# An attention and MLP block on one core: the residual of three output chunks added by accumulating transfers, VectorE's exponential groups allowed to begin during gelu, and a new list of their places

## The chip, the cores and the metric

The kernel runs on one core of a Trainium2 chip (trn2). The metric is device time in microseconds (us), the median of several runs. Before the change it is 464.41 us (9 runs, 464.27 to 464.72). A core has TensorE (PE, matmuls), VectorE (DVE), ScalarE (ACT), GpSimd (POOL) and SyncE (SP, which here only issues transfers). Each engine works through its own list of instructions in order and waits for the others by semaphores.

## The reference, cut to what matters

```
x: [1, 2048, 448]                 # S = 2048 rows, D = 448
xn = layernorm(x)
s  = MHA(xn): 16 heads of 28; p = softmax(q k^T * 28**-0.5); (p v) merged @ wo
g  = silu(gelu(xn @ w1 + b1) @ w2 + b2)        # hidden size 1792
out = x + s * g                                # bfloat16
```

## The kernel before, in words

The 2048 query rows are cut into C = 4 chunks of 512, the 16 heads into G = 4 groups of four. A block is one head group with one chunk; there are 16, and block b has group b // 4 and chunk b % 4. A block has 64 score tiles m of 128 keys by 512 queries, one for each head and each of 16 key tiles; a tile fills one PSUM bank. Block 15 is cut further into parts of 256, 128 and 128 queries.

**The exponential of the scores is the bulk of the work, and two engines share it.** ScalarE does most tiles: TensorE writes the scores of the next unit into a ring of six PSUM banks (`t_score`, the matmul is recorded at L1210), in units that alternate between three banks (from bank 0) and two (from bank 4), and ScalarE turns a unit into bfloat16 probabilities in one instruction of 1536 or 1024 columns (`p_exps`, L1266). So the scores of a unit can start when the exponential two units earlier has left the banks. The destination is `P`, or, when they are free, pieces of `h` and `xnT`; the profile names the groups by these.

VectorE does the tiles named in `QUADS`: 33 numbers q, each for the four tiles m = 4q to 4q + 3. Such a group takes its scores from whatever single bank is free (one of the pool: `misc`, `acc`, ring bank 3 or 2 at times); VectorE evicts each of the four (L1366), and then makes the exponential of the group out of integer and float16 operations on 2048 columns (`p_expq`, L1417 to L1424: three of about 0.69 us and two of about 1.22 us). A late score is either joined to a score burst that is due anyway (it then uses rows of the array that the burst leaves free) or issued by itself. The P·V matmuls (`pv_task`, L1478) accumulate in the bank `acc`, with VectorE's groups slipped in when they are ready.

**Beside this run** the projections of q, k and v for later groups (L734, L1021), the first MLP layer (L1062, L1079) and, from the middle on, gelu (`p_gelu`, L1117). In the gelu stretch ScalarE stops taking exponentials and alternates between pieces of `h` in SBUF and seven direct pieces of three PSUM banks each, which TensorE fills in the score ring (`p_direct`). Then follow the second layer (L1138, evicted with its bias by L1143), silu as a tanh (L1153) and a product (L1157), which leave `g` in `h`.

**When a block ends**, `p_epi` copies `acc` (L1536), sums with a matmul (L1543), takes the reciprocal (L1546, tile `rc`), splits it on POOL into a high and a low bfloat16 part (L1548 `rhi`, L1549 `rlo`), spreads it by a matmul (L1558) and multiplies (L1565). The last three parts of block 15 go through `p_epi4` and `p_norm4` instead: cast L1510, row sums by a matmul L1521, reciprocal L1524, product L1527.

**The output** of a chunk is made once its last block is normalised: `p_out` and `p_last` multiply with wo (`t_wo`, L1575, in parts of head groups), and `t_oev` finishes each 128-row tile on VectorE: times `g` (L1584), plus x (L1586), into `osb`, a part of `h`. The x for this comes from `x2`, another part of `h`, which SP loads again after silu of the chunk (L1162), because the first copy of x has been given to VectorE's groups as room. Chunks 0 to 2 leave by two transfers of two tiles each (L1592), chunk 3 by one for each tile (L1590), all issued on SP. For the last tile of chunk 3 silu is finished late: tanh on ScalarE after the last exponential (L1167), then a multiply and an add on POOL (L1169, L1171).

**What sets the order.** All of this is written by a planner in the kernel's own source, at build time: each strand of work is a generator that yields tasks (engine, buffers read and written, an assumed duration, a priority), and `run` always puts down the task that could start first by these durations, the priority deciding between near ones. What comes out is a fixed order for each engine. `p_late` decides when VectorE's groups start: group q waits for

```
K.next_m >= m0 - LEAD and len(K.banks) > 0 and K.unit_of(b, 3) is not None
```

where `next_m` is the next tile of ScalarE's stream, m0 = 4q and LEAD = 0. During gelu `next_m` stands still. `p_busy` (L895) puts filler matmuls into `acc` where the planner finds TensorE idle for too long.

Of the kernel before, what the change touches and what calls it, by code (L numbers as in the profile page):

```python
# [19 lines left out]
C = 4  # L20
# [7 lines left out]
MTOT = NBLK * T * 4  # L28

GM = 64 * 9 + 6  # L30
QUADS = (17, 19, 21, 35, 37, 50, 55, 68, 75, 84, 90, 102, 107, 116, 121, 133, 136, 146, 147, 149, 151, 162, 165, 179, 186, 195, 201, 209, 214, 218, 229, 235, 244)
SM_SCALE = DH ** -0.5
LOG2E = 1.4426950408889634
EXP_A3, EXP_A2, EXP_LC = 0.16391228, 0.00783292, 1.1187538523466403
# [9 lines left out]
SEM, OWN = 0.07, 0.03  # L44
SWITCH = 0.1
JOINT = 0.05
LEAD, WAIT = 0, 3.0
EPS = 0.1


# [23 lines left out]
class _Kernel:  # L74
# [183 lines left out]
    def alloc(self):  # L258
# [100 lines left out]
        self.b_fsb, self.b_sig = [B(), B()], [B(), B()]  # L359
        self.b_hf = [[B() for _ in range(FT)] for _ in range(C)]  # L360
        self.b_dum = B()
        hx = lambda c, f0, n: self.h[:, c, 512 * f0:512 * (f0 + n)].rearrange("p (k n) -> p k n", n=512)
        self.pslots = [(self.P[:, i0:i0 + n, :], k) for i0, n in ((0, NP),) for k in range(n)]
        self.pslots += [(hx(2, 5, 9), k) for k in range(9)] + [(hx(3, 0, 12), k) for k in range(12)]
# [218 lines left out]
    def loads(self):  # L583
        K = self

        def ld(dst, src, sem, w, land):
            return K.dma(SP, lambda eng: eng.dma_start(dst, src), sem, writes=w, land=land)
        xr = K.A_x[0].rearrange("(c p t) d -> c p t d", p=128, t=4)
        wq = K.A_wqkv
        ld(K.x_sb[:, 0, 0:2, :], xr[0][:, 0:2, :], K.s_x[0], [K.b_x0[0]], 3.2)  # L590
        K.dma(ACT, lambda eng: eng.dma_start(K.x_sb[:, 0, 2:4, :], xr[0][:, 2:4, :]), K.s_x0b, writes=[K.b_x0[1]], land=3.9)
        K.dma(ACT, lambda eng: eng.dma_start(K.x_sb[:, 1, :, :], xr[1]), K.s_x[1], writes=[K.b_x[1]], land=6.5)
        sv = K.stg.rearrange("p k w h d -> p k w (h d)")
        wqk = wq[:, 0:2 * D].rearrange("r (w n) -> r w n", w=2)

        def lw(n0, n1, sem, tok, land):
            for k in range(KT):
                rows = slice(128 * k, min(128 * k + 128, D))
                ld(sv[0:rows.stop - rows.start, k, :, n0:n1], wqk[rows, :, n0:n1], sem, [tok] if k == KT - 1 else [], land)
        lw(0, 4 * DH, K.s_w["wqk"], K.b_stg, 6.1)  # L600
        ld(K.wv[:, 0:3, 0:D], wq[0:384, 2 * D:3 * D].rearrange("(kt p) n -> p kt n", p=128), K.s_w["wv"], [], 0)
        ld(K.wv[0:64, 3, 0:D], wq[384:448, 2 * D:3 * D], K.s_w["wv"], [K.b_wv], 10.3)
        for c in (2, 3):
            ld(K.x_sb[:, c, :, :], xr[c], K.s_x[c], [K.b_x[c]], 8.0 + 1.8 * c)
        lw(4 * DH, D, K.s_wqk1, K.b_stg1, 16.5)

        ld(K.b2b[:, :], K.B_b2.partition_broadcast(128), K.s_w["b"], [K.b_b2], 20)
        ld(K.w1[:, 0:3, :], K.B_w1[0:384, :].rearrange("(kt p) f -> p kt f", p=128), K.s_w["w1"], [], 0)
        ld(K.w1[0:64, 3, :], K.B_w1[384:448, :], K.s_w["w1"], [K.b_w1], 30)

        def late_w2():
            yield ("until", lambda: K.next_m >= 64 * 2 * C and all(u in K.free_u for u in (4, 5, 6)))
            K.free_u = [u for u in K.free_u if u not in (4, 5, 6)]
            for u in (4, 5, 6):
                for b in K.b_U[u]:
                    K.b_w2.r += b.r + [b.w]
            ld(K.w2[:, :, :], K.B_w2.rearrange("(ft p) d -> p ft d", p=128), K.s_w["w2"], [K.b_w2], K.now + 14)
        K.spawn(late_w2(), 50)

        def pool_pads():  # L620
            yield ("until", lambda: K.stg_done == 2)
            yield _Task(POOL, lambda eng: eng.memset(K.wo[:, :, :], 0.0), [], [K.b_wo], 1.6)
            K.wait(SP, K.b_wo.w)
            K.b_wo.w = None
            for hh in range(H):
                g, j = hh // 4, hh % 4
                ld(K.wo[32 * j:32 * j + DH, g, :], K.A_wo[hh * DH:(hh + 1) * DH, :], K.s_w["wo"],
                   [K.b_wo] if hh == H - 1 else [], 45)
        K.spawn(pool_pads(), 50)
# [518 lines left out]
    def p_silu(self, c):  # L1148
        K = self
        yield ("until", lambda: K.f2n[c] == 4 and K.ready([K.b_fsb[c % 2]], 0.3) and (c < 2 or K.g_done[c - 2]))  # L1150
        fb, sg = K.fsb[:, c % 2, :, :], K.sig[:, c % 2, :, :]
        nt = 4 if c < C - 1 else 3
        yield _Task(ACT, lambda eng: eng.activation(sg[:, 0:nt, :], fb[:, 0:nt, :], ACTF.Tanh, scale=0.5),  # L1153
                    [K.b_fsb[c % 2]], [K.b_sig[c % 2]], 0.1 + 0.375 * nt, 0.0, 0)
        for t0 in range(0, nt, 2):
            t1 = min(t0 + 2, nt)
            yield _Task(DVE, lambda eng, t0=t0, t1=t1: eng.scalar_tensor_tensor(  # L1157
                K.g_sb[:, c, t0:t1, :], sg[:, t0:t1, :], 1.0, fb[:, t0:t1, :], op0=ALU.add, op1=ALU.mult),
                        [K.b_sig[c % 2], K.b_fsb[c % 2]], [K.b_h[c], K.b_g[c]], 0.15 + 0.467 * (t1 - t0), 0.0, 3)
        K.g_done[c] = True  # L1160
        K.b_x2[c].r = list(K.b_h[c].r) + [K.b_h[c].w]
        K.dma(SP, lambda eng: eng.dma_start(K.x2[:, c, :, :], K.A_x[0].rearrange("(c p t) d -> c p t d", p=128, t=4)[c]),  # L1162
              K.s_x2[c], writes=[K.b_x2[c]])
        if nt < 4:
            yield ("until", lambda: K.exp_m == MTOT - 1)
            o = K.g_sb[:, c, 3, :]
            yield _Task(ACT, lambda eng: eng.activation(sg[:, 3, :], fb[:, 3, :], ACTF.Tanh, scale=0.5),  # L1167
                        [K.b_fsb[c % 2]], [K.b_sig3], 0.47, 0.0, 0)
            yield _Task(POOL, lambda eng: eng.tensor_tensor(o, sg[:, 3, :], fb[:, 3, :], ALU.mult),  # L1169
                        [K.b_sig3, K.b_fsb[c % 2]], [K.b_h[c], K.b_g3], 0.85, 0.05, 0)  # L1170
            yield _Task(POOL, lambda eng: eng.tensor_tensor(o, o, fb[:, 3, :], ALU.add),  # L1171
                        [K.b_fsb[c % 2]], [K.b_h[c], K.b_g3], 0.85, 0.05, 0)
# [151 lines left out]
    def join(self, r):  # L1324
# [8 lines left out]
        p["task"].fn, p["task"].reads, p["task"].writes = t.fn, t.reads, t.writes  # L1333
        p["task"].dur, p["task"].rows = t.dur, t.rows

    def p_late(self):
        K = self
        yield ("until", lambda: K.late_on)
        K.spawn(K.p_room(), 0)
        for q in QUADS:  # L1340
            m0 = 4 * q
            b = K.sub_of(m0)
            yield ("until", lambda: K.next_m >= m0 - LEAD and len(K.banks) > 0 and K.unit_of(b, 3) is not None)
            u = K.unit_of(b)
            K.free_u.remove(u)
            ms = list(range(m0, m0 + 4))
            left = list(ms)
            for k in range(4):
                bank, tok = yield ("bank",)
                r = {"bank": bank, "tok": tok, "left": left, "m": None, "done": False}  # L1350
                still = lambda: (K.gu is not None and K.exp_u >= K.gu - 1 and K.dir_read < len(DIRECT)) or K.next_m >= MTOT or K.now > t0 + WAIT
                t0 = max(K.now, tok.tr, tok.tw or 0.0)
                yield ("until", lambda: K.may_join(r) or still())
                if K.may_join(r):
                    K.join(r)
                    yield ("until", lambda: r["done"])
                else:
                    r["m"] = left.pop(0)
                    yield K.t_score([r["m"]], {r["m"]: bank}, [tok], 0.9)
                K.spawn(K.p_apass(u, m0, r["m"] - m0, bank, tok), m0)  # L1360
            K.spawn(K.p_expq(m0, u), m0)
# [218 lines left out]
    def t_oev(self, ps, tok, c, t):  # L1580
        K = self
        o = K.osb[:, c, t, :]
        wr = K.b_osb[c][t // 2] if c < C - 1 else K.b_o4[t]
        yield _Task(DVE, lambda eng: eng.tensor_tensor(o, ps, K.g_sb[:, c, t, :], ALU.mult),  # L1584
                    [tok, K.b_g3 if (c, t) == (C - 1, 3) else K.b_g[c]], [wr], 0.63, 0.0, 3)
        yield _Task(DVE, lambda eng: eng.tensor_tensor(o, o, K.x2[:, c, t, :], ALU.add),  # L1586
                    [K.b_x2[c], wr], [wr], 0.4, 0.0, 3)
        ov = K.out[0].rearrange("(c p t) d -> c p t d", p=128, t=4)[c]
        if c == C - 1:
            K.outs.append(K.dma(SP, lambda eng: eng.dma_start(ov[:, t, :], o), K.s_out[6 + t], reads=[wr]))  # L1590
        elif t % 2:
            K.outs.append(K.dma(SP, lambda eng: eng.dma_start(ov[:, t - 1:t + 1, :], K.osb[:, c, t - 1:t + 1, :]),  # L1592
                                K.s_out[2 * c + t // 2], reads=[wr]))

    def p_out(self, c, t):
        K = self
        bank, tok = yield ("bank", lambda: K.on_done[(G - 1) * C + c] and K.g_done[c])
# [68 lines left out]
```

## Time and profile before

| | |
|---|---|
| median of 9 runs | 464.41 us |
| the profiled execution, its own time | 464.32 us |
| its span in the profile | 462.5 us |
| granted TensorE clock, mean | 0.998 |
| exponentials of 1536 columns on ScalarE (L1266) | 166, about 1.5 us each in the profile |
| exponentials of 1024 columns on ScalarE (L1266) | 197, about 1.07 us each |
| gelu stretch on ScalarE | 250.3 to 277.3 us |
| evictions of VectorE's groups (L1366) | 0.69 us each |
| residual adds on VectorE (L1586) | 16, 0.39 us in the median |
| output products on VectorE (L1584) | 16, 0.62 us |

A duration in the profile runs from the start of an instruction to its end, and the next one on the engine can start before that end; so the distance of two starts is the better price of an exponential. Idle time before an instruction is shown in square brackets with what ended it. "<-" separates what is written from what is read. POOL's and the transfers' queues have their own rows (SPq, ACTq). In the list of groups, three numbers in a row stand for the shortest, the median and the longest of them, in ns.

### The profile page before, as it was taken

To read this page: it belongs to the slowest core of one execution; us is meant where nothing else is said; L and a number is where in the kernel's file an instruction comes from. 1 tells how busy PE (TensorE), PEld (TensorE's weight loads), DVE (VectorE), ACT (ScalarE), POOL (GpSimd) and SP (SyncE) were. 2 spreads that over 40 slices of the span, in tenths; PEclk is the share of its full clock that TensorE was granted. 3 is DMA by queue.
4 is the path that set the end of the run, shared out by engine and by line. 5 is a ranking of instruction groups with operands and counts; after the bars stand their busy time and mean duration, and the time that the engine had idled before them with its cause. 6 is when DMAs were issued, how large, how long until landed. Compare 5 with 4: busy or idle time off the path is not lost.

```text
span 462.5 us, 10781 instructions
## 1 busy us (share of the span) xinstructions
PE 435.2 (94%) x4524; PEld 169.6 (37%) x4555; DVE 372.4 (81%) x588; ACT 448.3 (97%) x407; POOL 37.8 (8%) x79
## 2 busy tenths in 40 slices
PE   5999999999999899999999999999999999999995
PEld 4533333333323232323233343333333344343562
DVE  8956898898879797988888844889469698888796
ACT  6999999999999999999999999999999999999994
POOL 7470000001000000100000010000000001000001
PEclk9999999999999999999999999999999999999999
DMA  8501000000000000000040000101000010100001
GB/s 266 148 2 37 2 1 0 3 1 3 2 1 1 0 3 1 2 1 2 1 140 1 1 1 0 42 2 41 0 10 32 1 41 4 40 1 21 23 23 61
DMA packets 8385, 11.17 MB, mean 24 GB/s; under 512 B 1697, under 2 KB 6993, under 8 KB 8338
## 3 DMA queue, kind: packets, MB, share of 16 engines
q1 hardware_dynamic: 8050, 9.80, 6.9%
q8 instruction: 36, 0.59, 0.5%
q10 hardware_dynamic: 288, 0.69, 0.4%
q14 instruction: 11, 0.09, 0.1%
HBM read 8.61 MB, written 1.84 MB: 23 GB/s over the span
## 4 chain that ended last, share of the span: by engine, by line
PE 51%; ACT 36%; issue 10%; DVE 3%; DMA 1%; POOL 0%; ACTq 0%; DVEq 0%; POOLq 0%
ACT P L1266 17%; PE ring L1210 14%; ACT h L1266 12%; PE acc L1478 10%; ACT xnT L1266 6%; PE ring L1079 6%; PE misc L1138 5%; PE ring L1138 4%; PE acc L895 3%; PE misc L1079 2%; PE ring L734 2%; PE misc L734 1%; PE misc L1210 1%; PE ring L1575 1%; DMA x_sb<-in_A_x_dram 1%
## 5 line engine op out<-in xcount | busy, mean ns | idle before, releaser
L1266 ACT ACTIVATE P<-ring 128x1024 bf16<-128x1024 f32 (+1 forms) x194 | 222.0, 1256 | 1.8 <-PE ring L1210 0.9
L1210 PE MATMUL ring<-qT,kT 32*128 32x512 bf16 (+2 forms) x1088 | 143.7, 358 | 12.9 <-ACT P L1266 5.5
L1266 ACT ACTIVATE h<-ring 128x1024 bf16<-128x1024 f32 (+1 forms) x97 | 114.3, 1290 | 0.2
L1210 PEld LDWEIGHTS ring<-qT,kT 32*128 32x128 bf16 x1088 | 37.1, 91 | 132.6 <-ACT P L1266 53.6
L1266 ACT ACTIVATE xnT<-ring 128x1536 bf16<-128x1536 f32 (+1 forms) x72 | 83.5, 1282 | 0.2 <-PE misc L1210 0.2
L1478 PE MATMUL acc<-P,vaug 128*32 128x512 bf16 (+2 forms) x535 | 47.5, 358 | 0.0
L895 PE MATMUL acc<-ident,zero 128*128 128x128 bf16 x525 | 41.5, 220 | 0.0
L1079 PE MATMUL ring<-xnT,w 128*128 128x512 bf16 x149 | 39.1, 381 | 1.4 <-issue 1.0
L1548 POOL CAST rhi<-rc 128x16 bf16<-128x16 f32 x15 | 6.6, 440 | 389.2 <-DVE rc L1546 344.3
L895 PEld LDWEIGHTS acc<-ident,zero 128*128 128x128 bf16 x525 | 29.7, 98 | 17.6 <-issue 16.8
L1138 PE MATMUL misc<-w,h 128*128 128x448 bf16 x126 | 30.1, 355 | 0.0
L1478 PE MATMUL acc<-h,vaug 128*32 128x512 bf16 x241 | 25.1, 384 | 0.0
L1210 PE MATMUL misc<-qT,kT 32*128 32x512 bf16 (+1 forms) x64 | 24.1, 379 | 0.0
L1138 PE MATMUL ring<-w,h 128*128 128x448 bf16 x98 | 22.3, 354 | 0.1
L1366 DVE TENSOR_SCALAR x_sb<-ring 128x512 uint16<-128x512 f32 x22 | 15.2, 689 | 7.6 <-PE ring L1210 7.2
L1536 DVE CAST E_sb<-acc 128x512 bf16<-128x512 f32 x15 | 10.4, 692 | 13.2 <-PE acc L1478 13.0
L1079 PEld LDWEIGHTS ring<-xnT,w 128*128 128x128 bf16 x160 | 12.8, 97 | 18.7 <-issue 5.2
L1478 PE MATMUL acc<-xnT,vaug 128*32 128x512 bf16 (+2 forms) x240 | 18.2, 330 | 0.0
L1079 PE MATMUL misc<-xnT,w 128*128 128x512 bf16 x57 | 16.9, 382 | 0.9 <-issue 0.8
L1366 DVE TENSOR_SCALAR w<-ring 128x512 uint16<-128x512 f32 x20 | 13.8, 688 | 4.0 <-PE ring L1210 4.0
L1478 PEld LDWEIGHTS acc<-P,vaug 128*32 128x32 bf16 x535 | 11.9, 95 | 13.8 <-issue 10.2
L1117 ACT ACTIVATE h<-h 128x2560 bf16<-128x2560 bf16 (+2 forms) x8 | 16.6, 2072 | 0.0
(278 smaller groups left out, 654.9 us busy)
## 6 DMA issues: line engine op xcount, KB each, us to landing
h<-in_A_x_dram SPq DMA_DIRECT2D x4, 448.0 KB, 3.3
w<-in_B_w_dram SPq DMA_DIRECT2D x1, 1568.0 KB, 7.2
w<-in_B_w_dram SPq DMA_DIRECT2D x1, 1344.0 KB, 9.2
out_dram<-h SPq DMA_DIRECT2D x6, 224.0 KB, 1.9
x_sb<-in_A_x_dram SPq DMA_DIRECT2D x2, 448.0 KB, 4.7
h<-in_A_wqkv_dram SPq DMA_DIRECT2D x3, 168.0 KB, 4.7
x_sb<-in_A_x_dram ACTq DMA_DIRECT2D x1, 448.0 KB, 4.2
out_dram<-h SPq DMA_DIRECT2D x4, 112.0 KB, 1.7
```

The costliest lines, as they stand in the source:

```text
L734: ins = eng.matmul(bank, w[:, kt, g * 128:(g + 1) * 128], K.xnT[:, kt, c * 512:(c + 1) * 512], start=(kt == 0), stop=(kt == KT - 1))
L895: ins = eng.matmul(K.acc[:, 0:128], K.zero[:, :], K.ident[:, :], start=False, stop=True, skip_group_check=True)
L1079: ins = eng.matmul(bank, K.w1[:, kt, ft * 128:(ft + 1) * 128], K.xnT[:, kt, c * 512:(c + 1) * 512], start=(kt == 0), stop=(kt == KT - 1))
L1117: yield _Task(ACT, lambda eng, dst=dst, src=src: eng.activation(dst, src, ACTF.Gelu_apprx_tanh), rd, K.b_hf[c][f0:f0 + n] + ([K.b_h[c]] if ...
L1138: ins = eng.matmul(ps, hv[:, ft, t * 128:(t + 1) * 128], K.w2[:, ft, :], start=(ft == 0), stop=(ft == FT - 1))
L1210: return eng.matmul(dst, K.kT[32 * j:32 * j + 32, g, t * 128:(t + 1) * 128], K.qT[32 * j:32 * j + 32, g, c * 512 + q0:c * 512 + q0 + nq], ...
L1266: return eng.activation(reg[:, i0:i0 + n, :], K.ring[:, b0:b0 + n, :], ACTF.Exp, scale=SM_SCALE)
L1366: yield _Task(DVE, lambda eng: eng.tensor_scalar(K.unit[u][:, 512 * k:512 * k + 512].bitcast(dt.uint16), bank, SM_SCALE * LOG2E * 128.0, ( ...
L1478: return eng.matmul(K.acc[32 * j:32 * j + 32, q0:q0 + nq], K.vaug[:, t, 4 * g + j, :], ap[:, col:col + nq], tile_position=(0, 32 * j), sta ...
L1536: yield _Task(DVE, lambda eng: eng.tensor_copy(E, K.acc[:, :]), [K.b_acc], [tE], 0.7, 0.0, 0)
L1548: yield _Task(POOL, lambda eng: eng.tensor_copy(K.rhi[:, :], K.rc[:, :]), [K.b_rc], [K.b_rhl], 1.1, 0.0, 1)
L1575: ins = eng.matmul(ps, K.qT[:, g, c * 512 + t * 128:c * 512 + (t + 1) * 128], K.wo[:, g, :], start=(g == 0), stop=(g == G - 1))
```

## The change

- For chunks 0 to 2, `t_oev` no longer adds x, and `p_silu` no longer loads it into `h`. Instead `loads` has a new strand `out_x`, which has SP copy these three chunks of x straight from the input to the output in HBM; and the output transfers of these chunks go from SP to POOL's queue, with an addition into what the destination holds. Chunk 3 keeps its load and its adds.
- A group of VectorE may start up to GLEAD = 32 tiles ahead of `next_m`, where the gelu stretch (`in_gelu`) holds the ring.
- The 33 places in `QUADS` are others; their number in each block is the same.

As the planner lays out everything anew, many instructions change places on TensorE and VectorE, from about the third block on. The line numbers of the changed kernel are higher by up to 13 (L1266 becomes L1276, L1584 becomes L1597, L1586 becomes L1601, L1592 becomes L1605).

```diff
-QUADS = (17, 19, 21, 35, 37, 50, 55, 68, 75, 84, 90, 102, 107, 116, 121, 133, 136, 146, 147, 149, 151, 162, 165, 179, 186, 195, 201, 209, 214, 218, 229, 235, 244)
+QUADS = (17, 22, 24, 35, 36, 50, 55, 66, 75, 85, 89, 97, 106, 116, 118, 132, 139, 147, 148, 149, 151, 163, 173, 178, 186, 193, 201, 209, 216, 222, 225, 235, 242)
...
-LEAD, WAIT = 0, 3.0
+LEAD, WAIT, GLEAD = 0, 3.0, 32
...
+        self.b_ox = [B() for _ in range(C)]
...
+        def out_x():
+            yield ("until", lambda: K.late_on)
+            for c in range(C - 1):
+                ov = K.out[0].rearrange("(c p t) d -> c p t d", p=128, t=4)[c]
+                ld(ov, xr[c], K.s_x2[c], [K.b_ox[c]], K.now + 6)
+        K.spawn(out_x(), 50)
...
         K.g_done[c] = True
+        if c < C - 1:
+            return
         K.b_x2[c].r = list(K.b_h[c].r) + [K.b_h[c].w]
...
+    def in_gelu(self):
+        return self.gu is not None and self.exp_u >= self.gu - 1 and self.dir_read < len(DIRECT)
...
-            yield ("until", lambda: K.next_m >= m0 - LEAD and len(K.banks) > 0 and K.unit_of(b, 3) is not None)
+            yield ("until", lambda: K.next_m >= m0 - (GLEAD if K.in_gelu() else LEAD) and len(K.banks) > 0 and K.unit_of(b, 3) is not None)
...
-        yield _Task(DVE, lambda eng: eng.tensor_tensor(o, o, K.x2[:, c, t, :], ALU.add),
-                    [K.b_x2[c], wr], [wr], 0.4, 0.0, 3)
         ov = K.out[0].rearrange("(c p t) d -> c p t d", p=128, t=4)[c]
         if c == C - 1:
+            yield _Task(DVE, lambda eng: eng.tensor_tensor(o, o, K.x2[:, c, t, :], ALU.add),
+                        [K.b_x2[c], wr], [wr], 0.4, 0.0, 3)
             K.outs.append(K.dma(SP, lambda eng: eng.dma_start(ov[:, t, :], o), K.s_out[6 + t], reads=[wr]))
         elif t % 2:
-            K.outs.append(K.dma(SP, lambda eng: eng.dma_start(ov[:, t - 1:t + 1, :], K.osb[:, c, t - 1:t + 1, :]),
-                                K.s_out[2 * c + t // 2], reads=[wr]))
-
+            K.outs.append(K.dma(POOL, lambda eng: eng.dma_start(ov[:, t - 1:t + 1, :], K.osb[:, c, t - 1:t + 1, :],
+                                                                accum_op=ALU.add),
+                                K.s_out[2 * c + t // 2], reads=[wr, K.b_ox[c]]))
```

More of the change, by code (lines that the diff above doesn't have):

```diff
@@ L1350, in p_late @@
                 r = {"bank": bank, "tok": tok, "left": left, "m": None, "done": False}
-                still = lambda: (K.gu is not None and K.exp_u >= K.gu - 1 and K.dir_read < len(DIRECT)) or K.next_m >= MTOT or K.now > t0 + WAIT
+                still = lambda: K.in_gelu() or K.next_m >= MTOT or K.now > t0 + WAIT
                 t0 = max(K.now, tok.tr, tok.tw or 0.0)
```

## The prediction, made before the changed kernel had run

> **What bounds it now.** I read the page first: the busy row, then the chain that ended last.
>
> ```profile
> span 462.5 us, 10781 instructions
> ...
> PE 435.2 (94%) x4524; PEld 169.6 (37%) x4555; DVE 372.4 (81%) x588; ACT 448.3 (97%) x407; POOL 37.8 (8%) x79
> ```
>
> ScalarE is busy 97% of the span. Its idle 14.2 us lie at the ends: about 6 us before the first exponential at 12.67 us, and 6.8 us after its last instruction at 455.65 us. TensorE's 94% contains 525 filler matmuls (L895), so it has room. ScalarE's list of waits says what it still waits for:
>
> ```profile
> ACT P L1266 <- PE ring L1210: 0.9, 3, 0.5
> ...
> ACT P L1266 <- PE misc L1210: 0.7, 1, 0.7
> ...
> ACT h L1117 <- PE ring L1079: 0.4, 1, 0.4
> ```
>
> These are us in total, times, longest. From the first exponential to the last they come to about 2 us. Shorter waits are below that view's threshold; ScalarE's timeline shows them in the starts:
>
> ```profile
> 227.66 2.40 ACT L1266 ACTIVATE P<-ring 128x1536 bf16<-128x1536 f32 x2
> 230.72 4.62 ACT L1266 ACTIVATE P<-ring 128x1536 bf16<-128x1536 f32 x4 [0.67 <-PE misc L1210]
> ```
>
> Two exponentials should start the next one after 1.33 + 0.90 us, at 229.90; it started at 230.72. I took all start-to-start distances of the 363 exponentials: most often 904 ns (1024 columns) and 1331 ns (1536). What is above these is 7.2 us. So VectorE's work is off the path until the last exponential; the change can win or lose only (a) part of those 7.2 us, (b) the 0.4 us in gelu, (c) the end.
>
> The end, from the timeline of all engines:
>
> ```profile
> 448.26 6.94 ACT L1266 ACTIVATE xnT<-ring 128x1024 bf16<-128x1024 f32 x6
> ...
> 454.97 0.68 ACT L1167 ACTIVATE w<-w 128x448 bf16<-128x448 bf16 x1
> ...
> 455.74 1.03 POOL L1169 TENSOR_TENSOR h<-w 128x448 bf16<-128x448 bf16 x1 [17.92 <-ACT w L1167]
> ...
> 456.02 0.29 DVE L1510 CAST E_sb<-acc 128x128 bf16<-128x128 f32 x1 [0.21 <-PE acc L1478]
> 456.10 0.73 PE L1575 MATMUL ring<-wo,qT 128*128 128x448 bf16 x3
> 456.23 0.78 DVE L1586 TENSOR_TENSOR h<-h 128x448 bf16<-128x448 bf16 x1
> ...
> 456.67 0.22 PE L1521 MATMUL ring<-E_sb,selb 128*128 128x128 bf16 x1
> 456.85 1.06 POOL L1171 TENSOR_TENSOR h<-h,w 128x448 bf16<-128x448 bf16 x1
> 456.94 0.61 DVE L1584 TENSOR_TENSOR h<-misc,h 128x448 bf16<-128x448 f32 x1
> 457.47 0.94 DVE L1524 RECIPROCAL w<-ring 128x128 f32<-128x128 f32 x1
> 458.52 0.29 DVE L1527 TENSOR_TENSOR qT<-E_sb,w 128x128 bf16<-128x128 bf16 x1
> ```
>
> After the last exponential (ends 455.20) comes one chain: last P·V, cast L1510, row sums L1521, reciprocal L1524, L1527, projection, L1584, L1586 (ends 460.32), transfer, end at 462.5. Two things lengthen it: L1521 stands behind three projection matmuls on TensorE, and the reciprocal, whose input was there at 456.89, waits for an L1586 and an L1584 until 457.47.
>
> **The change, part by part.** The order of instructions of the built kernels settles what the diff does not. ScalarE has the same work in both: 197 exponentials of 1024 columns, 166 of 1536, the same gelu and tanh pieces, since there are 33 VectorE groups before and after. Only places move. So no part shortens ScalarE's 448.3 us.
>
> *Residual.* VectorE loses 12 adds L1586 at 0.39 us: 4.7 us, worth nothing between 385 and 455 us, where ScalarE is busy 69.98 of 70 us. SP loses three loads into h and six output issues, and gains three transfers x to out. These have no wait: SP issues them after the weights, at about 9.6 us, at about 0.5 us each, and SP's next work is at 35.26 (wo). They move 1.4 MB behind w1 on the same queue; at the 208 GB/s of the first 23 us that is 7 us, 13 if read and write both count, done before 35 us. Zero; if that cover were gone, wo would be late, which is read only from about 395 us.
>
> POOL gains six accumulating transfers, an operation that this trace doesn't show. By the order, each group's reciprocal split (rhi, rlo) stands behind two of them on POOL, and the in-order TensorE waits for rlo. In the tightest place (block 14) VectorE has, from the release of the first to the reciprocal that rhi needs, 0.62 + 0.68 + 1.22 + 0.62 (release of the second) and then 0.68 + 1.22 + 5 x 0.69 + 0.26: 8.7 us. The pair is free below 4.3 us an issue. Bounds: below, zero (it cannot gain, POOL has 8% to do); above, the delay by VectorE. The nearest row is POOL's own small cast:
>
> ```profile
> L1548 POOL CAST rhi<-rc x15: 198/199/1083, 49.1 to 437.3; 128x16 bf16<-128x16 f32 x15
> ```
>
> Minimum, median, maximum ns: the same 16 columns take 0.2 us alone and 1.08 beside VectorE. The Trainium skill speaks against the change here: "SBUF — State Buffer", section "SBUF: two separate sides", says that VectorE's two-port operations lock GpSimd out, so that it cannot write the descriptors of transfers that it issues; its section "A bandwidth-pool intuition that's wrong" gives about 0.62 us for such a transfer alone and 3.1 overlapped. By the row a pair holds POOL for 2.2 us, by the rule about 6.2 (an estimate): both below 8.7, so zero on the path by either. I take the row and keep 0 to +2 us. At the end POOL's multiply L1169 stands behind the last two issues; by the order their data is there before the score burst that starts at 446.46, and L1169 is needed at 455.7: 9 us of cover.
>
> *Groups in gelu.* In both orders eight or nine late scores stand in the gelu stretch, so the new condition moves little. Before the third direct piece (the one that waits 0.4 us) TensorE has 0.44 us less: two late scores (0.22 each) have gone behind it. That takes the 0.4. Later, before the last direct piece, two late scores (0.44), one P·V of 12 (0.64) and the broadcast (0.53) are new: with six pairs of 0.43 that is 4.2 us from the release at 269.6, so 273.8 against 274.9. Each late score also waits for VectorE's eviction of the one before (0.69 + latencies, about 1.1 us, against 1.07 us of spacing). Gain 0 to 0.4, loss up to 0.5: I take −0.2. The second layer's first seven pairs (0.37 each, 2.6 us) move from gelu's end into the exponential stream, and the four tanh come 5 to 9 exponentials later, still some 60 before their users: zero, apart from the windows below.
>
> *Other places.* I laid TensorE's work between two score bursts (0.213 us per 512 columns) against the stalls: before an exponential of 1536 columns a stall appears above about 1.05 us. Before: 32 such windows, 3.3 us above the mark, 3.75 us stalled. After: 27 windows, also 3.3 us, but in fewer, bigger lumps (1.59 and 1.81 us at exponentials 116 and 250; the 1.49 before 230.7 us is gone). The other 3.5 us of stalls have no such cause and stay. So 0, kept from −1 to +1.2.
>
> *The end.* In the new order the last two chunk-2 adds are gone, L1521 comes directly after the last P·V, and nothing stands between cast and reciprocal. From 456.02: cast 0.29, +0.06, L1521 0.22, +0.04, reciprocal 0.94 to 457.57; gap 0.11, L1527 0.29, +0.06, projection 0.36, +0.04, product 0.62, +0.04, add 0.39: 459.48 instead of 460.32, −0.84. But L1527 would run at 457.68 while POOL has L1171 until 457.91. L1586 took 0.78 beside POOL, against 0.39 otherwise, so I let the two exclude each other. Then L1527 starts at 457.95: −0.57. I take −0.55, from −0.84 to +0.2: the new cast stands behind the add of tile 2, which by the rows (its projection ends at 454.84) starts at 454.84 + 0.04 + 0.66 = 455.54, only 0.2 us before POOL's multiply at 455.74; if it comes second it waits out that multiply, the cast slips from 456.02 to 457.05 and the gain turns into +0.2.
>
> Sum: −0.55 (end) −0.2 (gelu) −0.1 (VectorE relieved where stalls wait for its evictions; an estimate from the 0.2 us stalls near 399 and 424) + 0 = −0.85. The profiled execution took 464.32 us, 1.85 more than its span, and is 0.09 below the median 464.41. 464.41 − 0.85 = 463.6.
>
> **Rivals.** *The stream improves too (20%).* If the lumps are better covered than the mark says, another 1 us of 7.2 goes: 462.5. For: before, 104 and 198 with 1.28 stalled nothing. Against: equal sums.
>
> *It does nothing (20%).* The add loses the race at the end (+0.75 on my sum), or the two lumps stall in full (0.5 and 0.8) while the other windows stall as before: 464.4 to 464.9. For: a 0.2 us margin. Against: the add's input comes from TensorE, whose order there is hardly changed.
>
> *Slower: POOL's issue (15%).* If an issue takes 6 us beside VectorE, a pair takes 12 where 8.7 are free: rhi is 3.3 us late, the broadcast blocks TensorE in order, the scores behind it stop ScalarE: 463.6 + 3.3 = 466.9. It costs from 4.3 us an issue and makes the kernel slower from 5.2. For: VectorE is busy 59.8 of 70 us there. Against: the worst stretched POOL row is 1.2 us.
>
> *Main case (45%):* 463.6, itself 462.9 to 464.3.
>
> **Numbers.** About 0.2% (0.93 us) is what a measurement can tell from no change. Faster by more means under 463.5: nearly half of the main case and the first rival, 0.42. Slower means over 465.3: 0.18. Within: 0.40. The range 462.2 to 465.9 leaves out some 5% below and 8% above.
>
> **What would show it.** ScalarE busy within 0.3 of 448.3 and the last exponential at 455.2 ± 0.8: right on the stream. From its end to the last add 4.5 us instead of 5.1: right on the end. No wait above 0.3 us of L1117. POOL transfers followed at once by rhi without TensorE waiting for rlo. Wrong if the last exponential ends before 454 or after 456.5, if POOL's transfers appear in the chain, or if the gap between span and time grows.

## The result and the profile after

The changed kernel takes 462.88 us (median of 9 runs, 462.74 to 463.01) against 464.41 us: ratio 0.9966, 95% interval 0.9958 to 0.9975. That is 1.53 us or 0.33% faster; the prediction was 463.6 us, with 462.9 to 464.3 as its main case.

The page's span and busy row, and its rows of transfers (KB each, median us from issue to landing):

```profile
span 460.9 us, 10748 instructions
...
PE 434.1 (94%) x4509; PEld 169.5 (37%) x4543; DVE 368.5 (80%) x576; ACT 448.2 (97%) x407; POOL 45.4 (10%) x85
...
out_dram<-in_A_x_dram SPq DMA_DIRECT2D x3, 448.0 KB, 10.5
out_dram<-h POOLq DMA_DIRECT2D x6, 224.0 KB, 3.8
```

ScalarE's busy time is what it was (448.2 against 448.3 us), so the 1.5 us are idle time of ScalarE that is gone. Measured on the two traces, they divide so (line numbers are those of the changed kernel):

| us | before | after | difference |
|---|---|---|---|
| first exponential starts | 12.67 | 12.60 | −0.07 |
| gelu, from the start of the exponential before it to the one after it | 29.76 | 29.39 | −0.37 |
| exponential stream outside gelu: starts late by over 30 ns, summed | 7.25 | 7.14 | −0.11 |
| what is left of the stream, mostly delays under 30 ns | | | −0.23 |
| last exponential's end to the last add's end | 5.12 | 4.38 | −0.74 |
| last add's end to the span's end | 2.15 | 2.13 | −0.02 |

The first row lies within chance: over the profiles of this study the first exponential starts between 12.55 and 13.13 us. In gelu, the 0.4 us wait of a direct piece is gone: ScalarE's list of waits has no row of that line any more. In the stream the sum hardly moved, but its parts did: exponentials 100 to 212 lose 2.97 us before and 1.66 after, exponentials 213 to 299 1.33 before and 2.53 after. ScalarE's timeline of the changed kernel shows both sides:

```profile
227.03 6.15 ACT L1276 ACTIVATE P<-ring 128x1536 bf16<-128x1536 f32 x5
...
321.09 2.36 ACT L1276 ACTIVATE P<-ring 128x1536 bf16<-128x1536 f32 x2 [0.81 <-PE misc L1220]
```

Where the old kernel stopped at 230.72 us, five exponentials now run through; the new large stop is exponential 250 at 321.09 us. (The bracket gives idle time between recorded ends and starts; from start to start this one is 0.95 us late.)

The end, from the timeline of all engines:

```profile
454.76 0.39 DVE L1601 TENSOR_TENSOR h<-h 128x448 bf16<-128x448 bf16 x1
454.96 1.08 POOL L1179 TENSOR_TENSOR h<-w 128x448 bf16<-128x448 bf16 x1 [9.98 <-ACT w L1177]
455.15 0.29 DVE L1523 CAST E_sb<-acc 128x128 bf16<-128x128 f32 x1
...
455.50 0.23 PE L1534 MATMUL misc<-E_sb,selb 128*128 128x128 bf16 x1 [0.40 <-DVE E_sb L1523]
455.77 0.96 DVE L1537 RECIPROCAL w<-misc 128x128 f32<-128x128 f32 x1 [0.33 <-PE misc L1534]
456.12 1.03 POOL L1181 TENSOR_TENSOR h<-h,w 128x448 bf16<-128x448 bf16 x1
456.83 0.46 DVE L1540 TENSOR_TENSOR qT<-E_sb,w 128x128 bf16<-128x128 bf16 x1
...
457.35 0.36 PE L1588 MATMUL ring<-wo,qT 128*128 128x448 bf16 x1 [1.61 <-DVE qT L1540]
457.75 0.62 DVE L1597 TENSOR_TENSOR h<-ring,h 128x448 bf16<-128x448 f32 x1 [0.46 <-PE ring L1588]
```

Nothing stands between cast and reciprocal any more: the row sums L1534 start 0.06 us after the cast, and the reciprocal 0.04 us after them. The add of tile 2 (454.76) won its place before POOL's multiply by 0.2 us.

POOL's timeline at two of the three chunk ends:

```profile
425.78 1.03 POOL L1605 DMA_DIRECT2D out_dram<-h  x1 [8.62 <-DVE h L1597]
428.78 0.86 POOL L1605 DMA_DIRECT2D out_dram<-h  x1 [1.97 <-PE acc L903]
434.49 0.55 POOL L1561 CAST rhi<-rc 128x16 bf16<-128x16 f32 x1 [4.85 <-DVE rc L1559]
```

The six issues take 0.86 to 1.11 us each. Here `rhi` comes 4.9 us after the pair is done: it waits for the reciprocal, not for POOL.

### The profile page after: what moved, and what is told of

Read it like the earlier page. It is cut to its first block, busy times and chain, and to the rows that moved or that the text cites. A ratio compares the mean times of both kernels' runs of the same rounds, so it can differ in the third digit from the quotient of the medians.

```text
span 460.9 us, 10748 instructions
## 1 busy us (share of the span) xinstructions
PE 434.1 (94%) x4509; PEld 169.5 (37%) x4543; DVE 368.5 (80%) x576; ACT 448.2 (97%) x407; POOL 45.4 (10%) x85
## 4 chain that ended last, share of the span: by engine, by line
PE 48%; ACT 37%; issue 11%; DVE 3%; DMA 1%; POOL 0%; ACTq 0%; DVEq 0%; POOLq 0%
ACT P L1276 18%; PE ring L1220 14%; ACT h L1276 10%; PE acc L1491 10%; ACT xnT L1276 6%; PE misc L1146 5%; PE ring L1146 4%; PE ring L1087 3%; PE acc L903 3%; PE misc L742 2%; PE misc L1087 2%; ACT h L1125 2%; PE ring L742 1%; PE misc L1220 1%; DMA x_sb<-in_A_x_dram 1%
## 5 line engine op out<-in xcount | busy, mean ns | idle before, releaser
L1276 ACT ACTIVATE P<-ring 128x1024 bf16<-128x1024 f32 (+1 forms) x194 | 221.8, 1260 | 1.8 <-PE misc L1220 0.8
L1276 ACT ACTIVATE h<-ring 128x1024 bf16<-128x1024 f32 (+1 forms) x97 | 114.3, 1292 | 0.3 <-PE misc L1220 0.2
L1276 ACT ACTIVATE xnT<-ring 128x1536 bf16<-128x1536 f32 (+1 forms) x72 | 83.5, 1269 | 0.0
L1561 POOL CAST rhi<-rc 128x16 bf16<-128x16 f32 x15 | 7.8, 522 | 359.2 <-DVE rc L1559 266.9
L1087 PE MATMUL ring<-xnT,w 128*128 128x512 bf16 x132 | 35.1, 381 | 1.5 <-issue 1.0
L903 PEld LDWEIGHTS acc<-ident,zero 128*128 128x128 bf16 x513 | 29.2, 98 | 17.6 <-issue 16.5
L1379 DVE TENSOR_SCALAR x_sb<-misc 128x512 uint16<-128x512 f32 x29 | 20.0, 689 | 13.0 <-PE misc L1220 12.9
L1146 PE MATMUL misc<-w,h 128*128 128x448 bf16 x112 | 27.2, 355 | 0.0
L1220 PE MATMUL misc<-qT,kT 32*128 32x512 bf16 (+1 forms) x70 | 26.0, 376 | 0.3 <-DVE qT L1578 0.3
L1146 PE MATMUL ring<-w,h 128*128 128x448 bf16 x112 | 26.0, 355 | 0.0
L1087 PE MATMUL misc<-xnT,w 128*128 128x512 bf16 x70 | 20.0, 381 | 1.3 <-issue 0.5
L1087 PEld LDWEIGHTS ring<-xnT,w 128*128 128x128 bf16 x144 | 11.3, 97 | 16.5 <-issue 5.3
L1379 DVE TENSOR_SCALAR x_sb<-ring 128x512 uint16<-128x512 f32 x19 | 13.0, 687 | 4.6 <-PE ring L1220 4.4
L1070 DVE CAST h<-misc 128x512 bf16<-128x512 f32 x20 | 13.8, 688 | 2.5 <-PE misc L1087 2.3
## 6 DMA issues: line engine op xcount, KB each, us to landing
out_dram<-in_A_x_dram SPq DMA_DIRECT2D x3, 448.0 KB, 10.5
```

Source lines behind the costliest of these rows:

```text
L903: ins = eng.matmul(K.acc[:, 0:128], K.zero[:, :], K.ident[:, :], start=False, stop=True, skip_group_check=True)
L1070: yield _Task(DVE, lambda eng: eng.tensor_copy(dst, bank), [tok], wr, 0.69, 0.0, 2)
L1087: ins = eng.matmul(bank, K.w1[:, kt, ft * 128:(ft + 1) * 128], K.xnT[:, kt, c * 512:(c + 1) * 512], start=(kt == 0), stop=(kt == KT - 1))
L1146: ins = eng.matmul(ps, hv[:, ft, t * 128:(t + 1) * 128], K.w2[:, ft, :], start=(ft == 0), stop=(ft == FT - 1))
L1220: return eng.matmul(dst, K.kT[32 * j:32 * j + 32, g, t * 128:(t + 1) * 128], K.qT[32 * j:32 * j + 32, g, c * 512 + q0:c * 512 + q0 + nq], ...
L1276: return eng.activation(reg[:, i0:i0 + n, :], K.ring[:, b0:b0 + n, :], ACTF.Exp, scale=SM_SCALE)
```

## The experiments

The change has three parts: the residual, the early start, the list of places. The first four runs and the sixth take some of them away; the others test a mechanism each. The new list alone was not run. A is in each expectation my own theory at that time; the other letters are the rivals that the same text spells out. Stalls are start-to-start delays of the exponential stream. As the planner lays out each of these kernels anew, a run shows what a part is worth in one layout.

### The residual alone

Old places and no early start; the residual as in the change:

```diff
+QUADS = the list of before
-LEAD, WAIT, GLEAD = 0, 3.0, 32
+LEAD, WAIT, GLEAD = 0, 3.0, 0
```

> The kernel before with the residual part alone (copies of x to the output, accumulating transfers, no adds on VectorE for chunks 0 to 2); old places, no early start in gelu. Theory A (what counts is where the planner's new order puts TensorE's and VectorE's work; relieving VectorE by itself is worth nothing): its order has the stream of before up to exponential 300, then two new lumps of TensorE work before an exponential of 1536 columns (2.19 us at 324, 1.39 at 344, mark 1.05: +1.4 us of stalls), and at the end one projection still stands before the row sums and one product between cast and reciprocal (about -0.4): 465.4 us, 464.6 to 466. Rival B (the 4.7 us taken from VectorE are the gain): 463.0, at most 463.3.

465.89 us, ratio 1.003 (1.002 to 1.0041): slower than before, and within A's range. The end is short already, 4.44 us; the stream loses 2.5 us in new stalls of 1.32 and 0.39 us at the ends of blocks 13 and 14 (exponentials 324 and 344, as A had counted) and of 0.81 us between them (exponential 337, which A had not). ScalarE's timeline at the largest:

```profile
412.04 1.45 ACT L1276 ACTIVATE P<-ring 128x1536 bf16<-128x1536 f32 x1 [1.01 <-PE ring L1220]
```

TensorE there has 32 P·V matmuls of the ending block (409.75 to 411.66 us) before the scores that this exponential needs. So the short end isn't bought by the new list, and the residual change by itself doesn't make the kernel faster.

### Residual and early start, old places

```diff
-QUADS = (17, 22, 24, 35, 36, ...
+QUADS = (17, 19, 21, 35, 37, ...
```

> The changed kernel with the old 33 places: residual part and early start in gelu, old list. Theory A: thirteen late scores instead of nine stand in the gelu stretch, the third direct piece still waits 0.4 us; at exponential 306 TensorE has 4.5 us of fillers and scores before the next burst, that is ScalarE stands still for some 3.4 us for a group of VectorE; 1.44 and 1.81 us lumps at 338 and 356 (+0.4, +0.75); the end is the new one (-0.7): 464.4 + 3.4 + 1.1 - 0.7 = 468.2 us, 467 to 469. Rival B: 463. Rival C (the early start in gelu is the gain): below 464.0.

471.92 us, ratio 1.0161 (1.0147 to 1.0175): the direction of A, but over its range. Gelu takes 31.10 us, and one stall alone costs 5.4 where A had counted 3.4:

```profile
397.11 1.45 ACT L1276 ACTIVATE xnT<-ring 128x1536 bf16<-128x1536 f32 x1 [5.30 <-PE acc L1491]
```

VectorE's last operation of the block's last group (L1437) ends at 395.61 us; only then can the last P·V, the cast (397.06) and the next block's work follow. ScalarE waits for VectorE's group here, through TensorE.

### New places and early start, VectorE adds x

The changed kernel with loads, adds and output transfers of all chunks as before:

```diff
-K.spawn(out_x(), 50)
...
+        yield _Task(DVE, lambda eng: eng.tensor_tensor(o, o, K.x2[:, c, t, :], ALU.add), ...
```

> The changed kernel without the residual part: new places and early start in gelu, but VectorE adds x for all chunks, with the loads and outputs of before. Theory A: the stream is that of the changed kernel to about exponential 310, then lumps of 1.44 and 1.55 us at 354 and 356 (+0.9 us against the changed kernel) and an end like that of before (a projection before the row sums, a product between: +0.6): 462.9 + 1.5 = 464.4 us, 463.8 to 464.9. Rival B gives 464.4 too, with the loss spread over the stream between 385 and 455 us and not in these two places; rival C: 463.2 or less.

465.93 us, ratio 1.003 (1.0019 to 1.0041): slower than A thought. The stream is that of the changed kernel until about exponential 310; from exponential 300 on it stalls 3.77 us instead of 0.80. The timeline of all engines at one block end:

```profile
415.53 1.23 DVE L1431 TENSOR_TENSOR kT<-kT,x_sb 128x2048 f16<-128x2048 bf16 x1
415.68 1.45 ACT L1273 ACTIVATE P<-ring 128x1536 bf16<-128x1536 f32 x1 [0.70 <-PE acc L1488]
...
416.67 0.68 DVE L1546 CAST E_sb<-acc 128x512 bf16<-128x512 f32 x1
...
418.02 1.02 ACT L1273 ACTIVATE P<-ring 128x1024 bf16<-128x1024 f32 x1 [0.89 <-PE acc L1488]
```

Both exponentials wait for P·V matmuls (L1488). The first waits for the last ones of the ending block; these include a group whose last operation on VectorE runs from 412.94 to 414.16 us, in the changed kernel from 410.23. The second waits for the first ones of the next block, which can't begin until a cast has emptied `acc`, and that cast stands on VectorE behind another group's 1.23 us operation. VectorE's timeline of the changed kernel has the cast ahead of the same operation:

```profile
412.94 0.69 DVE L1549 CAST E_sb<-acc 128x512 bf16<-128x512 f32 x1 [0.15 <-PE acc L1491]
413.55 1.22 DVE L1434 TENSOR_TENSOR kT<-kT,x_sb 128x2048 f16<-128x2048 bf16 x1
```

Taking the residual off VectorE is worth 3 us with these places. The end is 4.61 us here, with all adds on VectorE.

### Residual and new places, no early start

```diff
-LEAD, WAIT, GLEAD = 0, 3.0, 32
+LEAD, WAIT, GLEAD = 0, 3.0, 0
```

> The changed kernel with GLEAD = 0: new places, residual part, no early start in gelu. Theory A: block 9 has four groups of VectorE work (four evictions of 0.69 and 4.5 us of arithmetic each, 7.3 us a group, 29 us), and with the new list none of them may start before gelu ends; ScalarE runs out of room for probabilities at exponential 238 and stands still until VectorE is through: a gap of 20 to 33 us, 483 to 496 us. Rival D (the early start moves little, since the orders have eight and nine late scores in gelu): 463 to 464.

500.17 us (one run). A had the direction and was 4 us short. ScalarE's waits, then VectorE's busy time (third group of numbers after the stretch's length: DVE) between 250 and 300 us in this kernel:

```profile
ACT w L1161 <- DVE w L1151: 32.5, 3, 15.3
ACT P L1276 <- PE acc L1491: 5.6, 1, 5.6
```

```profile
250.00:300.00 50.00, 48.62 (x345) 18.98 (x342) 17.15 (x25) 49.95 (x38) 0.41 (x2) 1.00 0.01 1
```

and in the changed kernel:

```profile
250.00:300.00 50.00, 48.70 (x362) 17.85 (x363) 33.62 (x45) 49.93 (x38) 0.42 (x2) 1.00 0.01 2
```

Without the early start VectorE does 16.5 us less in this stretch, and all of that stands after it, mixed with the bias evictions L1151 that the tanh L1161 on ScalarE waits for. The kernel before, with other places, was busy 32.90 us there without any early start.

### The same, without the planner's standing back

In the run above VectorE also idled: its evictions came 4.4 us apart, and I took the planner's WAIT for the cause.

```diff
-LEAD, WAIT, GLEAD = 0, 3.0, 0
+LEAD, WAIT, GLEAD = 0, 0.0, 0
```

> The run without the early start (500.2 us, ScalarE idle some 38 us between 306 and 350 us), now with the planner's WAIT, the longest time that a late score may stand back for a score burst to join, at 0 instead of 3.0 us. In the run with 3.0, evictions of VectorE's groups came 4.4 us apart in that stretch, with VectorE idle between. Theory A (the gap is the planner's own: each late score stands back 3 us for a burst that can't come, because ScalarE's next instruction is a tanh that waits for VectorE behind these evictions): most of the gap goes, 465 to 478 us. Rival D (the new places give VectorE more than it can do after gelu, if nothing starts early): the gap stays above 25 us, 488 us or more.

490.40 us, ratio 1.0559 (1.0546 to 1.0573). My theory fell; the rival held. ScalarE's waits and the stretch:

```profile
ACT w L1161 <- DVE w L1151: 19.1, 2, 16.0
ACT P L1276 <- PE acc L1491: 9.3, 2, 6.7
```

```profile
306.00:331.00 25.00, 24.04 (x160) 9.94 (x162) 22.47 (x31) 4.10 (x3) 0.00 (x0) 1.00 0.00 1
```

VectorE is busy 22.5 of 25 us while ScalarE works 4.1. Standing back made some 10 us of the 37; the rest goes with VectorE's backlog.

### The early start alone

```diff
-LEAD, WAIT = 0, 3.0
+LEAD, WAIT, GLEAD = 0, 3.0, 32
```

> The kernel before with only the early start (GLEAD = 32 in gelu); old places, residual on VectorE for all chunks. With the old places and the residual by transfers the early start gave 471.9 us: gelu 31.1 us instead of 29.8, and a stall of 5.4 us at exponential 306, where a block's end waited for the last of VectorE's groups. In the built order of this kernel a lump of 4.5 us of TensorE work stands before exponential 306 again. Theory A (early start and old places do not fit, whoever adds x): gelu 31.1 us, a stall above 3 us at exponential 306, 469.5 us (467.5 to 472). Rival (it was the residual change that spoiled it): 464.4 us or less, no stall above 1.5 us.

475.55 us, ratio 1.0242 (1.0229 to 1.0255). As A said, gelu takes 31.11 us and exponential 306 is late by 5.4 us; the same stall as with the residual change, so that one didn't cause it. The time is beyond A's range by a further stall of 2.3 us at exponential 326 and an end of 7.0 us, where four products with their adds (468.0 to 472.0 us) queue on VectorE. Why the planner, with the old places, lays out gelu and the end of block 12 so badly once groups may start early was not settled.

### Chunk 2's residual back on VectorE

```diff
-            for c in range(C - 1):
+            for c in range(C - 2):
...
-        if c == C - 1:
+        if c >= C - 2:
```

> The changed kernel, but chunk 2 gets its x from VectorE again (its load, four adds and two plain output transfers on SP as before); chunks 0 and 1 keep the accumulating transfers. In the built order the four adds stand between the four chunk-2 products (one every 1.19 us near 440 to 443 us, with 0.57 us idle between), ahead of the last cast by over 10 us, and the last cast, row sums and reciprocal stand as in the changed kernel. Theory A (the end became shorter because the order there is another, not because adds were saved): 462.9 us (462.7 to 463.2), from the last exponential to the last add 4.4 us. Rival B (saved VectorE work at the end is itself the gain): 463.6 us, end 5.0 us or more.

463.05 us, ratio 0.9972 (0.9962 to 0.9983), end 4.47 us: as A said. The end became shorter because the order there is another; the four saved adds are not needed for it. (Of its 4.47 us, 0.1 is a projection matmul L1588 of 0.46 instead of 0.36 us.)

### Plain output transfers on SP

```diff
-            K.outs.append(K.dma(POOL, ..., accum_op=ALU.add), K.s_out[2 * c + t // 2], reads=[wr, K.b_ox[c]]))
+            K.outs.append(K.dma(SP, ...), K.s_out[2 * c + t // 2], reads=[wr]))
```

> The changed kernel with the six output transfers of chunks 0 to 2 as plain ones on SP; it leaves out the residual of these chunks (the copies of x to the output are still made, and are overwritten). Theory A (accumulating on POOL costs nothing on the path): 462.9 us, within 0.2. Rival (POOL's issues at 0.86 to 1.11 us each hold rhi and rlo, or stretch VectorE's work): faster by 0.3 us or more, 462.6 or less, with fewer stalls after 390 us.

463.11 us, ratio 0.9974 (0.9963 to 0.9985); stalls 7.15 us, end 4.38 us. Accumulating, and issuing on POOL, costs nothing that this measurement can see.

### Twelve accumulating transfers

```diff
-        elif t % 2:
+        else:
             K.outs.append(K.dma(POOL, lambda eng: eng.dma_start(ov[:, t, :], K.osb[:, c, t, :], accum_op=ALU.add), ...
```

> The changed kernel with twelve accumulating transfers of one tile each on POOL instead of six of two tiles; everything else and the order are the same. This doubles POOL's issues (six more at 0.86 to 1.11 us). Theory A (POOL has room: a pair was free below 4.3 us an issue): within 0.2 us of the changed kernel, 462.9 us, each issue still about 0.9 us. Rival (issues are only just hidden, or stretch VectorE's two-source work): slower by 0.4 us or more, with new stalls after 390 us.

467.03 us, ratio 1.0065 (1.0051 to 1.0079): slower, with 3.7 us of new stalls after exponential 330. But the issues are no longer than before (0.86 to 1.10 us). Of all engines' waits this one is new:

```profile
DVE h L1598 <- DMA out_dram<-h: 6.5, 5, 2.2
```

The two tiles of a pair are one buffer to the program, so the second product waited until the first tile's transfer had been read out. What came onto the path is a transfer's landing, not POOL's issue. The run says nothing on the rival as it was meant; a version with a buffer for each tile wasn't tried.

### Without POOL's last add

```diff
-            yield _Task(POOL, lambda eng: eng.tensor_tensor(o, o, fb[:, 3, :], ALU.add), ...
```

> The changed kernel without POOL's last add (L1181, 1.03 us); it leaves out that term of silu for the last tile of chunk 3. The order is otherwise the same. My prediction let L1540 and that add exclude each other; in the changed kernel L1540 took 0.46 us beside it against 0.29 elsewhere. Theory A (sharing with POOL stretches VectorE's product, it does not wait for it): L1540 takes 0.29 us, from the last exponential to the last add 4.21 instead of 4.38 us, time 462.7 us. Rival (the 0.46 has another cause): end 4.38, time 462.9 us.

462.89 us, ratio 0.9968 (0.9957 to 0.998), end 4.37 us. The timeline of all engines:

```profile
456.97 0.29 DVE L1538 TENSOR_TENSOR qT<-E_sb,w 128x128 bf16<-128x128 bf16 x1
...
457.32 0.52 PE L1586 MATMUL ring<-wo,qT 128*128 128x448 bf16 x1 [1.45 <-DVE qT L1538]
```

The product takes 0.29 us instead of 0.46: the other 0.17 are POOL's add. But the projection after it took 0.52 us instead of 0.36. The row of the microsecond from 457 to 458 (the third number from the right is the granted clock), here and then in the changed kernel:

```profile
457.00:458.00 1.00, 0.52 (x1) 0.10 (x1) 0.39 (x2) 0.00 (x0) 0.00 (x0) 0.70 0.00 0
```

```profile
457.00:458.00 1.00, 0.36 (x1) 0.10 (x1) 0.54 (x2) 0.00 (x0) 0.14 (x1) 1.00 0.00 0
```

In every one of the fourteen profiles the granted clock goes from 1.00 to 0.50 once near the end. In ten of them it does so after this projection, which then takes 0.36 us. In four (this one at 457.4 us, the one with chunk 2 on VectorE, and both without the early start) it does so before the projection ends, which takes 0.46 to 0.55 us. So in this profile the clock took what POOL's add had cost. The median of 462.89 us didn't fall either; at what moment the clock went down in the runs that were not profiled isn't known, nor what sets the moment.

### Other places against the lump at exponential 250

I looked for lists without the lump of TensorE work before exponential 250. The first moves two groups by a few tiles, the second six (its expectation says seven):

```diff
-..., 163, 173, 178, 186, 193, 201, 209, 216, 222, 225, 235, 242)
+..., 163, 171, 179, 186, 193, 201, 209, 216, 222, 225, 235, 242)
```

> The changed kernel with only two other places: 173 becomes 171, 178 becomes 179. Sum above the mark of 1.05 us 2.56 instead of 3.32, the lump at exponential 250 gone. Theory A: 462.1 us (461.8 to 462.4), the stall of 0.95 us near 321 us gone. Rival B (the stall moves or block ends are hit): 462.7 or more.

462.00 us, ratio 0.9954 (0.9941 to 0.9966), the fastest kernel of this study. Its ScalarE runs through where the changed kernel stopped:

```profile
315.63 8.23 ACT L1276 ACTIVATE P<-ring 128x1536 bf16<-128x1536 f32 x7
```

Part of the stall comes again later: exponential 261, at 335.22 us, is late by 0.63 us instead of 0.19, waiting for the P·V of a block's end. All in all the stream's stalls fall from 7.14 to 6.42 us. The count of work above the mark had fallen by 0.76.

```diff
-..., 163, 173, 178, 186, 193, 201, 209, 216, 222, 225, 235, 242)
+..., 163, 171, 179, 185, 194, 204, 209, 216, 222, 224, 235, 242)
```

> The changed kernel with seven other places: 173, 178, 186, 193, 201, 216 and 225 become 171, 179, 185, 194, 204, 222 dropped-in order, so that 171, 179, 186 to 242 read 171, 179, 185, 194, 204, 209, 216, 222, 224, 235, 242. By the count of TensorE's work before each exponential (mark 1.05 us) the lump of 1.81 us at exponential 250 is gone; the sum above the mark falls from 3.32 to 2.62. Theory A (a lump stalls ScalarE for what it is above the mark): the 0.95 us stall near 321 us goes and no other of that size comes: 462.2 us (461.9 to 462.5). Rival B (the stall only moves, or VectorE's work at the block ends is met at another point): 462.7 or more.

462.56 us, ratio 0.9963 (0.995 to 0.9975), just over A's range of 461.9 to 462.5; the five runs lie between 462.20 and 462.95. Stalls are 6.52 us, the 0.95 us stall gone, and 0.63 us again at exponential 261. In its profile the first exponential started at 12.93 us instead of 12.60, before anything in the list matters; without that it stands 0.2 us behind the run above.

## Why the prediction was right, and where it was not

The prediction counted its sum from the finished instruction orders of both kernels, and that sum came out well. What it said each part of the change is worth did not: two terms that it set near zero, the residual and the early start, cost 3 and 37 us when they are undone. The measured 462.88 us lies nearer to its first rival (462.5) than to its main figure.

**What bounds the kernel: right in the main, with one step wrong.** ScalarE's busy time is unchanged, and the gain lies in the places named: gelu, stream, end. But "VectorE's work is off the path until the last exponential" is refuted. ScalarE being busy 69.98 of 70 us says only that the layout of before had no wait there. With the new places, the residual of all chunks on VectorE, twelve adds more, costs 3 us (465.93 against 462.88), because a block's end needs VectorE's last operation and its cast in time. The four adds of chunk 2 alone cost no more than 0.2 us (463.05), so their place counts and not their number. That my −0.1 us for "VectorE relieved" agrees with the stream of the two whole layouts (0.11 gained in stalls, 0.23 in smaller delays) is luck; as the worth of the adds it was wrong.

**The end: right mechanism, one term mis-sized.** Predicted −0.55, measured −0.74. The add kept its place, and the chain ran as laid out. I let L1540 wait for POOL's add and then take its full 0.29 us, a loss of 0.27. It started at 456.83, POOL's add ended at 457.15, and L1540 ended at 457.29: a loss of 0.17, where its whole 0.29 us after that add would have lost 0.32. In the profile before, the add beside POOL's multiply did likewise: it ended at 457.01, 0.24 us after the multiply, where it takes 0.39 alone. In both, about 0.15 us less than the whole instruction was left when POOL was done. The Trainium skill ("SBUF — State Buffer", section "Who interferes with whom") has an instruction of VectorE with two inputs in SBUF blocked, not slowed, by GpSimd's reading. The rows agree with a wait; what I had wrong is that the whole instruction still stands behind it. The rest of the difference is the cast, 0.73 us after the last exponential instead of 0.82. I had named the adds of chunk 2 that are gone beside the order; the run with them back (end 4.47 us) shows that they aren't needed for the gain, and the run with the residual alone (4.44 us) that the new list isn't either.

**Gelu: right.** Predicted −0.2 between −0.4 and +0.5, measured −0.37. The added work before the last direct piece cost nothing. But I had put this gain under the early start, and it is the new list's: with the new places and no early start gelu takes 29.40 us, with the early start and the old places 31.10 (29.76 before, 29.39 after).

**The early start: wrong.** I wrote that "the new condition moves little", since late scores stand in gelu in both orders. They do, but with the new list they stand there only because of the condition: without it 16.5 us of VectorE's work moves out and the kernel takes 500 us. The condition and the list are one thing, and counting instructions in the two finished orders could not show that.

**The windows: right in sum, and nearly in size.** Predicted 0; measured −0.11. The two lumps stood 0.54 and 0.76 us above the 1.05 us mark and stalled 0.39 and 0.95 us. Taking one of them away gave 0.72 us where the count said 0.76.

**POOL's issue: refuted as a rival.** 0.86 to 1.11 us each, below 4.3 where it would begin to cost; plain transfers on SP are no faster. That the row of the small cast which I went by (1.08 us) was near is luck: the cast takes 0.20 us and waits for an operation of VectorE, while an issue takes 0.86 and 0.88 us with VectorE idle (both in the run with twelve transfers, at 446.10 and 443.71 us). "Beside VectorE" was also too wide: beside VectorE's work on PSUM the cast takes 0.20 us too. One of the six issues did wait: that at 425.78 ended 0.12 us after an operation of VectorE with one input that ran from 426.00 to 426.68. The figure of 3.1 us beside a copy on VectorE, from the Trainium skill ("SBUF — State Buffer", section "A bandwidth-pool intuition that's wrong"), did not appear here. On SP the three copies of x took 0.6 to 1.3 us each to issue where I had 0.5, and nothing waited for them.

**"The stream improves too"** happened in a mild form: 0.34 us outside gelu. I had 0.1 of it in the sum. The other 0.24, with the end and gelu terms, each better by 0.2 than I took, make up 0.6 of the 0.72 us between 463.6 and 462.88.

## What to carry to other kernels

An engine without waits in one layout can still have its price in another: test it by putting the work back in the new layout, as the residual here, which was worth nothing by the old profile and 3 us in the new kernel. Where a planner writes the order, parts of a change can't be priced one at a time: the five part-changes run here (the residual, the early start, and each pair of the three parts) were all slower than the kernel before, and all three parts together faster.

What can be counted beforehand is the bounding engine's next need: TensorE's work between two score bursts, against what an exponential covers. That gave the two large stalls of the changed kernel within 0.2 us and found a better list. It does not see what VectorE's lateness does: the 5.4 us stall with the old places was counted as 3.4, and the two stalls of 1.0 us with the adds back on VectorE were not foreseen.

## What was not expected of the hardware

- An accumulating transfer takes POOL 0.86 to 0.88 us to issue when VectorE is idle, and in most cases beside its work too (0.86 to 0.90). The first one takes 1.11 us in the profiles of all ten kernels that have them. Ten others take 0.95 to 1.18 us: there an operation of VectorE with one input and all its data in SBUF had begun 0.14 to 0.33 us after the issue, and the issue ended 0.08 to 0.13 us after that operation. Twelve transfers of half the size take as long each. One of 224 KB lands in 3.8 us (plain on SP, in the kernel before: 1.9), and a copy of 448 KB within HBM in 10.5 us.
- Of two instructions on POOL and VectorE with their data in SBUF, the second waits for the first, but less than its whole own time is then left. The timeline of all engines in the changed kernel shows the small cast of the reciprocal's split begin during an operation of VectorE:

```profile
415.65 1.16 DVE L1437 TENSOR_TENSOR kT<-kT,wk 128x2048 bf16<-128x2048 f16 x1
415.80 1.06 POOL L1561 CAST rhi<-rc 128x16 bf16<-128x16 f32 x1 [14.16 <-DVE rc L1559]
```

It ends 0.05 us after VectorE. Of the 210 such casts in the fourteen profiles, 117 began while VectorE worked with all its data in SBUF, and each ended 0.05 to 0.06 us after it; the other 93, with VectorE idle or at work on PSUM, took 0.20 us. The second instruction of the split, 0.22 us alone, ended 0.07 to 0.08 us after VectorE, the product of 128 columns, 0.29 us alone, 0.15 us after POOL's add, and the add of 448 columns, 0.39 us alone, 0.25 us after POOL's multiply. So each was done 0.14 or 0.15 us sooner than if all of it had come after the wait.

- VectorE's cast from PSUM (0.29) and the add that had begun before POOL's multiply (0.39) took no longer than elsewhere; that multiply, begun 0.2 us into the add, took 1.08 us instead of 1.03.
- Near the end of the program the granted clock goes from 1.00 to 0.50, between 1.4 and 4.1 us after the last matmul before the final projection. Where that is before the projection's end, its 0.36 us become 0.46 to 0.55 (four of fourteen profiles).
